# Lightning attention and a highway layer: weights loaded through an f32 staging tile late in the queue, five more idle products, and a re-written order

## The chip, the cores and the metric

The kernel runs on one core of one Trainium2 chip. The metric is the device time of one execution in microseconds (us), lower is better.

## What is computed

The reference is a block-wise decayed linear attention over `q`, `k`, `v` of shape (4 batches, 8 heads, 768 positions, 64) in f32, followed by a highway layer with two 512x512 weights. Cut to what matters:

```
for b in range(nb):                                  # blocks of 64 positions
    intra = (qb @ kb^T * Dmask) @ vb
    inter = (qb * lam_pow) @ kv_state
    out[block] = intra + inter
    kv_state = lam_block * kv_state + (kb * rev_pow)^T @ vb
x = out, heads side by side                          # 3072 x 512
H = relu(x @ w_h);  T = sigmoid(x @ w_t + b_t)
result = T * H + (1 - T) * x
```

## The kernel before

The work is cut into 12 steps (4 batches of 3 stretches of 256 positions; `n` is the step). The decay powers are folded into the operands: q is multiplied by `pow_q`, v by `pow_k`, both made once from `lam`. Each step has an attention part and a highway part.

Attention part of step n: q, k and v arrive as f32 by SyncE's queue (`load`, line 200; each DMA moves 256 KB, so a step has six). Three tasks bring them to bf16: `cast_k` (kinds `ck2`, `ck`), `scale` for q (`cq2`, `cq`) and for v (`cv2`, `cv`). TensorE turns k and q over (`trans`, `tr2`/`tr`, products with the identity, line 218), an engine copies the turned tile out of PSUM (`evac_h`, `et2`/`et`), TensorE makes scores (`scores`, `s`, line 234) in two halves u = 0, 1, VectorE masks them (`mask`, `m`, line 238), TensorE multiplies by v (`intra`, `a`, line 259), keeps the running state (`state`, `kv`, line 267; copied out by `ss`), and adds the state's share (`inter`, `i0`/`i`, line 247). `xT` copies the result out. Steps 0 and 1 are cut in two parts of four heads each (the kinds with a 2 at the end).

Highway part: `block` (kind `f`, line 288) multiplies by the weights `w_b` in bf16, eight products of 128x256 a task, four tasks a step; `hx`, `g` and `thD`/`thP` combine; `turn` (`x`, line 310) turns the result back by products with the identity, `eo` copies it out and `st` stores it.

Nothing is scheduled on the fly. The kernel makes a list of tasks in a fixed order, each of a kind with an engine (table `KINDS`, or for copies a letter of the strings in `EN`: A is ScalarE, V VectorE, G GpSimd), and the list `ORDER` says in which order they are issued. Every engine runs its tasks strictly in that order. Line 436 asserts that no task stands ahead of one that it depends on. PSUM is shared: the tag "w" has five buffers (`WB`) for turned tiles, scores, highway products and turned-back results; "o" and "kv" have one each. The f32 staging tiles of q, k and v have five buffers each from step 2 on (`LA`).

Two things around the change. First, the idle products: `fill` (line 191) issues two products of the identity with itself, 128x512 each, into the attention's PSUM tile; nothing reads them. There are `NF` = 12 such tasks; all stand at the head of TensorE's queue, before the first turn of step 0. Second, the weights: `load_w` (line 164) issues from GpSimd a DMA that reads f32 and writes bf16, half the columns of one weight each. There are four (kind `gw`); the kind `lw` is empty here. In `ORDER` three of them stand at the head of GpSimd's queue and the fourth behind step 0's `cv2` tasks. SyncE's queue begins: step 0 (six DMAs), q of step 1's first half, q of step 2, the rest of step 1, the rest of step 2, step 3, and so on, with no weight among them.

Of the kernel before, what the change touches and what calls it, by code (L numbers as in the profile page):

```python
# [8 lines left out]
F32 = mybir.dt.float32  # L9
# [11 lines left out]
class Task:  # L21
# [9 lines left out]


LETTER = dict(A="ACT", V="DVE", G="POOL")
KINDS = {"SP": "lw l l2 st st1 st3", "DVE": "m hx hx1 hx4 thD thD1 thD4 btc", "POOL": "gw thP thP1 thP4", "ACT": "g g1 g4 pow tab", "PE": "bt fill tr tr2 kv i i0 s a f f1 f4 x x1 x3"}
FIXED = {kind: eng for eng, kinds in KINDS.items() for kind in kinds.split()}
LA = 5
XB = 3
OB = 12
WB = 5
NF = 12  # L40
PARTS = 2
TH = ["DVE", "POOL"]
GROUPS = [[0], [1], [2], [3], [4], [5], [6], [7], [8], [9], [10]]
EN = dict(
    ck2="AVGV", cq2="GVGG", cv2="GGGG", et2="AVAAVAAA", ss="VAVVVAVAAVVAVVVAVAAA", xT="VAAAVAAVAAAAAAAAVVVAAAAV",
    eo="AVVAAAAVAAVVAVAVVAVVAV", ck="AAAGGAGAAA", cq="GGGGGGGGGG", cv="GGGGVGGGGG", et="AAAVAVAAAVAAAAAAAVAA", eo1="A", eo3="VA")
ORDER = [
    25, 26, 12, 36, 13, 24, 14, 0, 34, 15, 6, 8, 35, 16, 17, 18, 75, 2, 19, 9, 20, 125, 28, 21, 22, 74, 23, 29, 27, 32, 84, 33,
    39, 30, 31, 85, 37, 44, 38, 40, 41, 45, 4, 78, 42, 76, 43, 46, 82, 86, 47, 83, 128, 48, 124, 49, 126, 50, 77, 10, 1, 132, 56,
    51, 88, 133, 11, 80, 5, 52, 81, 55, 79, 92, 57, 99, 53, 93, 87, 3, 100, 89, 90, 54, 101, 91, 94, 127, 95, 7, 98, 102, 130,  # L50
    103, 163, 96, 129, 131, 104, 97, 105, 162, 58, 106, 107, 137, 59, 134, 164, 108, 135, 138, 63, 203, 139, 136, 64, 140, 110,
    109, 202, 141, 60, 111, 142, 65, 61, 166, 243, 143, 66, 62, 113, 112, 165, 67, 204, 115, 144, 114, 145, 168, 170, 116, 167,
    146, 242, 171, 169, 71, 68, 147, 206, 172, 244, 69, 72, 177, 153, 173, 178, 176, 179, 205, 117, 180, 280, 174, 210, 181, 154,
    151, 182, 246, 211, 183, 281, 208, 184, 175, 148, 209, 185, 207, 282, 250, 152, 149, 118, 186, 119, 251, 245, 320, 212, 150,
    121, 213, 187, 155, 217, 122, 214, 216, 218, 215, 321, 247, 220, 219, 188, 221, 248, 189, 222, 191, 361, 283, 249, 190, 156,
    223, 192, 157, 284, 255, 322, 252, 224, 286, 256, 225, 193, 253, 287, 257, 399, 233, 285, 194, 226, 234, 195, 254, 360, 227,
    323, 290, 258, 159, 291, 259, 196, 324, 160, 362, 288, 260, 197, 326, 289, 231, 327, 364, 439, 328, 232, 261, 329, 292, 295,
    199, 325, 293, 296, 398, 228, 262, 200, 263, 368, 297, 229, 271, 402, 400, 369, 230, 330, 294, 298, 331, 266, 272, 299, 363,
    440, 300, 264, 267, 235, 335, 265, 301, 438, 365, 332, 268, 269, 302, 336, 303, 366, 333, 479, 236, 442, 337, 367, 406, 270,
    334, 237, 370, 480, 338, 407, 239, 371, 273, 339, 304, 240, 340, 403, 309, 401, 478, 305, 274, 310, 404, 373, 275, 405, 73,  # L60
    341, 374, 311, 443, 342, 375, 446, 343, 276, 408, 312, 447, 372, 376, 277, 409, 441, 377, 482, 306, 238, 378, 344, 307, 278,
    351, 345, 201, 410, 308, 279, 352, 379, 411, 313, 241, 413, 444, 481, 380, 161, 346, 414, 483, 445, 198, 381, 349, 158, 415,
    347, 486, 70, 350, 382, 487, 123, 348, 412, 120, 448, 383, 353, 416, 484, 449, 417, 317, 485, 418, 314, 354, 315, 318, 419,
    450, 316, 453, 420, 355, 384, 319, 451, 454, 356, 421, 389, 455, 385, 488, 390, 452, 386, 456, 429, 489, 457, 458, 357, 430,
    491, 358, 459, 387, 492, 359, 460, 493, 461, 424, 388, 422, 425, 391, 490, 423, 494, 462, 426, 495, 392, 427, 496, 393, 497,
    428, 394, 467, 498, 463, 431, 501, 512, 395, 502, 468, 499, 464, 396, 500, 503, 397, 469, 465, 432, 470, 466, 506, 504, 433,
    507, 471, 435, 505, 434, 515, 436, 513, 508, 516, 472, 437, 514, 475, 517, 473, 520, 476, 518, 474, 521, 523, 477, 509, 519,
    524, 522, 510, 525, 526, 511, 527, 528]


@with_exitstack
def kernel(
# [11 lines left out]
    nc = tc.nc  # L84
# [4 lines left out]
    DM = H * D  # L89
    KC = DM // 128  # L90
# [4 lines left out]
    singles = ctx.enter_context(tc.tile_pool(name="singles", bufs=1))  # L95
# [32 lines left out]
    id_f = singles.tile([KC, KC], F32)  # L128
    nc.vector.tensor_copy(id_f, id128[0:KC, 0:KC])
    bt_col = singles.tile([128, KC], F32)  # L130
    w_b = [singles.tile([128, KC, DM], BF16, name=f"w_b{i}") for i in range(2)]
    wh, wt = w_b

# [5 lines left out]
    def buf(name, tag, shape, dtype=BF16, bufs=1, pool=None):  # L139
        made[name] = Tile(tag, bufs)  # L140
        made[name].make = lambda: (pool or sb).tile(shape, dtype, tag=tag, name=tag, bufs=bufs)
        return made[name]
# [7 lines left out]
    def task(kind, emit, reads=(), writes=(), after=(), only=()):  # L150
        eng = FIXED.get(kind)
        if eng is None:
            i = count.get(kind, 0)
            count[kind] = i + 1
            eng = LETTER[EN[kind][i]]
        t = Task(kind, eng, emit, [made[x] for x in reads], [made[x] for x in writes], after, only)
        tasks.append(t)
        return t

    V, A, P, T = nc.vector, nc.scalar, nc.gpsimd, nc.tensor  # L160
    ENG = {"DVE": V, "POOL": P}


    def load_w(w, y):
        nc.gpsimd.dma_start(out=w_b[w][:, :, y * 256:(y + 1) * 256],
                            in_=(moe_w_h, moe_w_t)[w].rearrange("(kc p) n -> p kc n", p=128)[:, :, y * 256:(y + 1) * 256])

    def copy(eng, dst, src):
        if eng == "ACT":
            A.activation(dst, src, AF.Copy)  # L170
        else:
            ENG[eng].tensor_copy(dst, src)  # L172

    w_done = {}
    for y, w in ((0, 0), (0, 1), (1, 0), (1, 1)):
        a = task("gw", lambda eng, w=w, y=y: load_w(w, y))
        w_done[w, y] = [task("lw", lambda eng: None, after=[a])]


    def powers(eng):  # L180
# [14 lines left out]
    buf(("fill",), "o", [128, 2, NP, C], F32, pool=ps)  # L195
    for i in range(NF):
        task("fill", fill, writes=[("fill",)])
# [81 lines left out]
    def group(n, b):  # L279
        for g in GROUPS:  # L280
            if n in g:
                return g[0], 2 * (n - g[0]) + b, 2 * len(g)
        return n + b, 0, 1
# [39 lines left out]
    for n in range(N):  # L323
        bt, c = divmod(n, NST)
        P2 = n < PARTS
        parts = [slice(0, 4), slice(4, 8)] if P2 else [slice(0, 8)]
        y = "2" if P2 else ""
# [58 lines left out]
        for b in range(2):  # L386
            g, r, z = group(n, b)
            y = {1: "1", 2: "", 4: "4"}[z]
# [9 lines left out]
            w = 1 if z == 4 else 2  # L398
# [24 lines left out]
            y = "3" if fin else "1"  # L423
# [45 lines left out]
```

## Time and profile before

| | |
|---|---|
| median of 3 runs | 119.93 us (119.2 to 120.29) |
| profiled execution, its own time | 120.29 us |
| its span, first to last instruction of the program | 118.2 us |
| TensorE busy (matmul) | 104.4 us, 88% of the span |
| VectorE / ScalarE / GpSimd busy | 79.8 / 71.0 / 65.0 us |
| moved by DMA | 26.52 MB, mean 224 GB/s |
| mean granted TensorE clock | 0.907 |

In profile lines PE is TensorE's matmul, PEld its weight load, DVE VectorE, ACT ScalarE, POOL GpSimd and SP SyncE; a q behind an engine's name is its instruction queue. A line number such as L234 is a line of the kernel above. In group lines the tile behind `<-` is what is read, `x16` is the number of instructions. PEclk is the share of TensorE's full clock that was granted.

### The profile page before, as it was taken

To read this page: it belongs to the slowest core of one execution; us is meant where nothing else is said; L and a number is where in the kernel's file an instruction comes from. 1 tells how busy PE (TensorE), PEld (TensorE's weight loads), DVE (VectorE), ACT (ScalarE), POOL (GpSimd) and SP (SyncE) were. 2 spreads that over 40 slices of the span, in tenths; PEclk is the share of its full clock that TensorE was granted. 3 is DMA by queue.
4 is the path that set the end of the run, shared out by engine and by line. 5 is a ranking of instruction groups with operands and counts; after the bars stand their busy time and mean duration, and the time that the engine had idled before them with its cause. 6 is when DMAs were issued, how large, how long until landed. Compare 5 with 4: busy or idle time off the path is not lost.

```text
span 118.2 us, 4773 instructions
## 1 busy us (share of the span) xinstructions
PE 104.4 (88%) x2073; PEld 87.0 (74%) x2073; DVE 79.8 (67%) x131; ACT 71.0 (60%) x128; POOL 65.0 (55%) x57
## 2 busy tenths in 40 slices
PE   5983226998999999999999999999999999999960
PEld 1432114776888988989989889889898888889950
DVE  0112324494396899898977779798899868795840
ACT  3564222363706975876978975968697866237650
POOL 7793034937400799998098999849463001230620
PEclk9998555555699999999999999999999999999997
DMA  0999999999999999999999999506494422022373
GB/s 19 272 214 216 242 260 298 284 279 296 286 295 290 290 291 287 288 286 294 284 271 293 303 295 288 178 24 243 168 371 179 175 105 89 6 89 89 119 284 134
DMA packets 43900, 26.52 MB, mean 224 GB/s; under 512 B 1764, under 2 KB 40936, under 8 KB 43880
## 3 DMA queue, kind: packets, MB, share of 16 engines
q1 hardware_dynamic: 41616, 25.17, 76.7%
q0 software_dynamic: 2112, 1.05, 6.6%
q8 instruction: 16, 0.26, 0.9%
q14 instruction: 4, 0.03, 0.1%
q10 hardware_dynamic: 152, 0.01, 0.1%
HBM read 20.98 MB, written 6.29 MB: 231 GB/s over the span
## 4 chain that ended last, share of the span: by engine, by line
PE 78%; DMA 9%; SPq 3%; POOL 2%; DVE 1%; ACT 1%; issue 1%; POOLq 1%
PE w L288 37%; PE w L218 11%; DMA qf<-in_q_dram 9%; PE w L310 9%; PE w L234 6%; PE o L259 5%; PE kv L267 5%; PE o L247 5%; SPq L203 3%; POOL qb L212 2%; POOLq L464 1%; DVE m L238 1%; ACT kT L170 1%; DVE hmx L292 0%; DVE ss L172 0%
## 5 line engine op out<-in xcount | busy, mean ns | idle before, releaser
L288 PE MATMUL w<-xT,w_b 128*128 128x256 bf16 (+1 forms) x416 | 47.6, 265 | 0.0
L288 PEld LDWEIGHTS <-w_b 128*128 128x128 bf16 x416 | 36.6, 98 | 4.7 <-issue 0.2
L238 DVE TENSOR_TENSOR m<-w,tri 128x512 bf16<-128x512 f32 x48 | 31.1, 684 | 6.2 <-PE w L234 6.0
L304 POOL TENSOR_TENSOR th<-t_sb,hmx 128x512 bf16<-128x512 bf16 (+1 forms) x13 | 14.0, 1079 | 33.2 <-DVE hmx L292 17.4
L212 POOL TENSOR_TENSOR qb<-qf,pow_q 128x1024 bf16<-128x1024 f32 (+1 forms) x13 | 22.1, 1702 | 9.7 <-DMA qf<-in_q_dram 6.5
L212 POOL TENSOR_TENSOR vs<-vf,pow_k 128x1024 bf16<-128x1024 f32 (+1 forms) x13 | 21.2, 1636 | 5.7 <-issue 3.2
L292 DVE SCALAR_TENSOR_TENSOR hmx<-w,xT 128x512 bf16<-128x512 f32 (+1 forms) x26 | 16.7, 647 | 5.8 <-PE w L288 4.3
L301 ACT ACTIVATE w<-w,bt_col 128x256 f32<-128x256 f32 (+1 forms) x26 | 11.2, 432 | 10.7 <-PE w L288 5.6
L170 ACT ACTIVATE kT<-w 128x1024 bf16<-128x1024 bf16 (+1 forms) x13 | 12.0, 925 | 6.6 <-PE w L218 6.6
L170 ACT ACTIVATE xT<-o 128x512 bf16<-128x512 f32 x17 | 9.5, 598 | 8.0 <-PE o L259 6.9
L310 PE MATMUL w<-id,th 128*128 128x128 bf16 x96 | 12.8, 219 | 0.6 <-POOL th L304 0.6
L234 PE MATMUL w<-qT,kT 64*64 64x128 bf16 x384 | 12.6, 234 | 0.7 <-ACT kT L170 0.7
L170 ACT ACTIVATE qT<-w 128x1024 bf16<-128x1024 bf16 (+1 forms) x9 | 7.9, 881 | 8.6 <-PE w L218 8.6
L310 PE MATMUL w<-id,xT 128*128 128x128 bf16 x96 | 12.8, 220 | 0.0
L218 PE MATMUL w<-id,qb 128*128 128x128 bf16 x96 | 8.7, 238 | 4.4 <-DVE qb L212 2.2
L301 ACT ACTIVATE t_sb<-w,bt_col 128x256 bf16<-128x256 f32 (+1 forms) x26 | 10.5, 457 | 2.1 <-PE w L288 2.0
L304 DVE TENSOR_TENSOR th<-w,hmx 128x512 bf16<-128x512 f32 (+1 forms) x13 | 8.3, 647 | 4.0 <-ACT w L301 3.6
L218 PEld LDWEIGHTS <-qb 128*128 128x128 bf16 x96 | 6.7, 106 | 5.6 <-POOL qb L212 2.6
L218 PE MATMUL w<-id,kb 128*128 128x128 bf16 x96 | 8.8, 238 | 1.7 <-ACT kb L170 1.5
L259 PE MATMUL o<-m,vs 64*64 64x128 bf16 x384 | 9.1, 233 | 1.1 <-DVE m L238 1.1
L310 PEld LDWEIGHTS <-th 128*128 128x128 bf16 x96 | 9.4, 98 | 0.8 <-POOL th L304 0.8
L234 PEld LDWEIGHTS <-kT 64*64 64x64 bf16 x384 | 8.5, 113 | 2.0 <-ACT kT L170 0.9
(45 smaller groups left out, 124.8 us busy)
## 6 DMA issues: line engine op xcount, KB each, us to landing
qf<-in_q_dram SPq DMA_DIRECT2D x24, 256.0 KB, 5.5
vf<-in_v_dram SPq DMA_DIRECT2D x24, 256.0 KB, 5.4
kf<-in_k_dram SPq DMA_DIRECT2D x24, 256.0 KB, 5.3
out_dram<-o_sb SPq DMA_DIRECT2D x23, 256.0 KB, 2.4
w_b<-in_moe_w_h_dram POOLq DMA_DIRECT2D x2, 256.0 KB, 8.3
w_b<-in_moe_w_t_dram POOLq DMA_DIRECT2D x2, 256.0 KB, 10.3
out_dram<-o_sb SPq DMA_DIRECT2D x2, 128.0 KB, 1.7
lam_bc<-in_lam_dram ACTq DMA_DIRECT2D x1, 4.0 KB, 3.5
```

Of the source, the lines that this page charges most:

```text
L170: A.activation(dst, src, AF.Copy)
L212: ENG[eng].tensor_tensor(dst[:, hs], in0=get(x, n, p).rearrange("p h (j d) -> p h j d", j=J), in1=pw[:, :, :, None].to_broadcast([128, hs. ...
L218: T.transpose(get(x + "tr", n, p)[:, i, j, :], get(x + "b", n)[:, j, h:h + 2, :], id128)
L234: T.matmul(get("s", n, u, e)[half(b), i, j, :], lhsT=turned("k", n)[half(e), hp, b * C + j:(b + 1) * C:J], rhs=turned("q", n)[half(e), hp, ...
L238: V.tensor_tensor(get("m", n, u)[:, e], in0=get("s", n, u, e), in1=tri[:, None].to_broadcast([128, 2, J, C]), op=ALU.mult)
L247: T.matmul(get("o", n)[half(e), b, hp, :], lhsT=get("ss", n, b)[half(e), hp, :], rhs=turned("q", n)[half(e), hp, b * C:(b + 1) * C], start ...
L259: T.matmul(get("o", n)[half(e), b, 2 * u + i, :], lhsT=get("vs", n)[half(b), 4 * u + 2 * i + e, j, :], rhs=get("m", n, u)[half(b), e, i, j ...
L288: T.matmul(get(x, g, js[0])[:, i, :], lhsT=w[:, kc, j * 128:(j + 1) * 128], rhs=get("xT", g)[:, kc, :], start=(kc == 0), stop=(kc == KC - 1))
L292: V.scalar_tensor_tensor(get("hmx", g, js[0]), in0=get("h", g, js[0]), scalar=0.0, in1=get("xT", g)[:, js[0]:js[-1] + 1, :], op0=ALU.max, ...
L301: A.activation(get(*gate(g, js))[:, i, :], get("t", g, js[0])[:, i, :], AF.Sigmoid, bias=bt_col[:, j:j + 1])
L304: ENG[TH[js[0] // len(js) % 2]].tensor_tensor(get("th", g)[:, js[0]:js[-1] + 1, :], in0=get(*gate(g, js)), in1=get("hmx", g, js[0]), op=AL ...
L310: T.matmul(get("x", n, b, p)[:, (j - js[0]) * 128:(j - js[0] + 1) * 128], lhsT=get(x, g)[:, j, r * C:(r + 1) * C], rhs=id128, start=(j == ...
```

## The change

The GpSimd DMAs go. Each weight is loaded as f32 into a staging tile `w_f` by four SyncE DMAs of 256 KB (128 partitions, two of four row blocks, half the columns), and eight tasks of kind `cw` copy the pieces to `w_b`: four on GpSimd, three on ScalarE, one on VectorE. In the new `ORDER` the eight loads stand on SyncE's queue behind all of steps 0, 1 and 2 and ahead of step 3.

`NF` is 17. Twelve idle products stand ahead of the first turn as before; the five others stand on TensorE's queue behind each of the four turns of step 0 and behind the first scores of step 0.

`ORDER` and the strings of `EN` are written anew throughout. For steps 0 and 1 the loads of SyncE are in the order v, k, q, q, k, v (step 0), q, k, k, q, v, v (step 1), then step 2. On GpSimd the first tasks are now step 0's second `cv2` and step 1's `cq2`, `ck2`, `cq2`; VectorE has `ck2`, `cv2`, `cq2`, `cq2` of step 0 at its head, and the `cv2` tasks of step 1 between the masks of step 0 and those of step 1.

The diff, the numbers of `ORDER` left out:

```
-KINDS = {... "SP": "lw l l2 st st1 st3", ... "POOL": "gw thP thP1 thP4", ...}
+KINDS = {... "SP": "lw l l2 st st1 st3", ... "POOL": "thP thP1 thP4", ...}
-NF = 12
+NF = 17
 EN = dict(
-    ck2="AVGV", cq2="GVGG", cv2="GGGG", et2="AVAAVAAA", ss="VAVVVAVAAVVAVVVAVAAA", xT="VAAAVAAVAAAAAAAAVVVAAAAV",
-    eo="AVVAAAAVAAVVAVAVVAVVAV", ck="AAAGGAGAAA", cq="GGGGGGGGGG", cv="GGGGVGGGGG", et="AAAVAVAAAVAAAAAAAVAA", eo1="A", eo3="VA")
+    cw="GVGGGAAA", ck2="VVGA", cq2="VVGG", cv2="VGVV", et2="VAAVAVAV", ss="AAVAAAAVAVAAAAVVAVAV", xT="VAVAAAAAAAAAAAAAAAAAAAAA",
+    eo="AVVAAAVAAVAVAVAAAAVAVA", ck="VAAGGAGVGG", cq="GVGGGGGGGG", cv="GGGGGGGGGG", et="AVAVAVVAVAAAAAAAAAAA", eo1="A", eo3="AA")
...
+    w_f = [singles.tile([128, KC, DM], F32, name=f"w_f{i}") for i in range(2)]
     w_b = [singles.tile([128, KC, DM], BF16, name=f"w_b{i}") for i in range(2)]
...
-    def load_w(w, y):
-        nc.gpsimd.dma_start(out=w_b[w][:, :, y * 256:(y + 1) * 256],
-                            in_=(moe_w_h, moe_w_t)[w].rearrange("(kc p) n -> p kc n", p=128)[:, :, y * 256:(y + 1) * 256])
+    def piece(x, y, i):
+        return x[:, 2 * i:2 * i + 2, y * 256:(y + 1) * 256]
+
+    def load_w(w, y, i):
+        nc.sync.dma_start(out=piece(w_f[w], y, i), in_=piece((moe_w_h, moe_w_t)[w].rearrange("(kc p) n -> p kc n", p=128), y, i))
...
     for y, w in ((0, 0), (0, 1), (1, 0), (1, 1)):
-        a = task("gw", lambda eng, w=w, y=y: load_w(w, y))
-        w_done[w, y] = [task("lw", lambda eng: None, after=[a])]
+        w_done[w, y] = []
+        for i in range(2):
+            a = task("lw", lambda eng, w=w, y=y, i=i: load_w(w, y, i))
+            w_done[w, y].append(task("cw", lambda eng, w=w, y=y, i=i: copy(eng, piece(w_b[w], y, i), piece(w_f[w], y, i)), after=[a]))
```

## The prediction

> **What bounds the kernel now.** I read the page first (busy shares, the 40 slices), then the windows, the chain of waits over the first 33 us, and the timeline there.
>
> ```profile
> PE   5983226998999999999999999999999999999960
> PEclk9998555555699999999999999999999999999997
> DMA  0999999999999999999999999506494422022373
> ```
>
> A slice is 2.96 us. From the eleventh slice to the last but two TensorE has no gap; before that it is mostly empty and at half clock, while the DMA engines are full from 3 us to 77 us. The windows, cut where the clock changed (columns: window, length, busy time and instructions of PE, PEld, DVE, ACT, POOL, clock, DMA share, GB/s):
>
> ```profile
> 7.59:11.01 3.42, 1.28 (x19) 0.70 (x21) 0.69 (x1) 1.40 (x3) 2.41 (x3) 1.00 1.28 214
> 11.01:14.42 3.41, 1.05 (x20) 0.54 (x16) 1.08 (x3) 0.60 (x1) 0.00 (x0) 0.50 1.27 238
> 14.42:17.83 3.41, 1.19 (x12) 0.73 (x15) 1.24 (x3) 0.60 (x1) 1.03 (x1) 0.50 1.23 256
> ...
> 21.25:24.66 3.41, 3.41 (x52) 2.53 (x56) 2.15 (x5) 1.70 (x3) 3.36 (x4) 0.50 1.08 284
> 24.66:28.07 3.41, 2.92 (x80) 2.47 (x74) 2.11 (x4) 2.38 (x4) 0.91 (x2) 0.50 1.04 280
> 28.07:31.49 3.42, 3.42 (x73) 2.76 (x66) 1.71 (x3) 1.46 (x2) 2.96 (x2) 0.50 1.13 295
> ```
>
> The clock was full until 11.0, half until 31.5, then full to the end. A window with PE busy 1.28 of 3.42 cost it; 3.41 of 3.41 in 21.25 to 24.66 did not yet bring it back. The chain names what the start waits for:
>
> ```profile
> 5.13 10.95 DMA qf<-in_q_dram
> 16.17 1.04 POOL qb L212
> ...
> 21.18 1.03 PE w L218 x8
> ...
> 32.24 0.35 PE w L234 x16
> ```
>
> A load of q for step 1, issued at 5.13, lands at 16.09. Between 5 and 18 us the four weight DMAs land too (10.59, 13.08, 15.47, 17.98 in the trace); they read 2 MB f32 in all. So steps 0 and 1 are starved by weights that no product reads before 30.9 us. Step 1's last load lands at 23.39, step 2's at 27.14, step 3's at 32.35.
>
> So the end is fixed by when TensorE becomes dense at full clock. From step 2's first scores (32.17) to the end of the span (118.24) it is 86.1 us, with one block of L288 (eight products, 0.87 in the chain) already done. The new order does that block later, so its span is the time of step 2's first scores plus 86.1 + 0.9 = 87.0, plus whatever is run at half clock behind them. The products are otherwise the same.
>
> **The change, part by part.** The sum is made against the profiled execution: span 118.24 and 2.05 around it, 120.29. The median 119.93 is 0.36 below that; I subtract 0.36 at the end.
>
> *Loads moved.* Without weights in front, loads land at the spacing that the trace has when loads are alone: 21.66, 22.53, 23.39, 24.23, so 0.87 us for 256 KB. The first lands at 5.16 as before. Then step 0 is complete at 9.5 (was 13.67), step 1 at 14.7 (was 23.39), step 2 at 19.9 (was 27.14), the eight weight pieces at 20.8 to 26.9, step 3 at 32.1 (was 32.35). From step 3 on the bytes ahead are equal, so nothing is lost there: SyncE has eight issues more, which cost 0.4 to 0.8 each and run while its queue waits for the full DMA engines. GpSimd loses four issues, 0.94 + 0.75 + 0.75 + 0.80 = 3.2 us, which stood ahead of its first casts.
>
> *Casts added.* Eight of 128x512 f32 to bf16. The rows for that shape (kb): GpSimd 0.61, ScalarE 0.63, VectorE 0.43, and 1.09 where GpSimd worked beside it. So GpSimd 2.4, ScalarE 1.9, VectorE 0.4 to 1.1. They stand between 21 and 28 us. The first highway block needs ScalarE's two (pieces landed at 20.8 and 21.7, done by about 25), and I have TensorE there at 25 to 27; the others are done at 23 to 28 and asked for at 28 or later. On the path: 0 (covered by the attention of step 2), up to 1 if that cover is gone. Behind the waiting ScalarE casts stand `xT` of step 1 and `ss` of step 2, 0.6 and 0.4; both have the same cover.
>
> *Idle products.* 24 of them took 6.7 us before; at full clock the later ones run at 0.21, so a `fill` of two is 0.43 and five are 2.15. They go into gaps that TensorE has anyway while ScalarE and VectorE copy (0.6 to 0.69 a copy). Walking the four turns: turns and fills alternate from 8.1 (end of the twelve) to 11.1, where the first scores start; without them about 10.2. Then the masks of step 0 and landings of step 1 (11.2 to 14.7) take over. Price on the path: 0 to 1, taken in the walk below.
>
> *The walk to step 2's first scores*, in row durations (VectorE: mask 0.64, turned tile 0.69 or 1.22, scale 0.69, copy of xT 0.69, ss 0.42; ScalarE 0.60, 1.02 and 0.38). At full clock: scores u=0 at 11.1, u=1 at 12; four masks on VectorE 11.75 to 14.35; `a` of step 0 at 14.6; one `et2` and two `cv2` that VectorE now does, and xT, to 17.2; `kv`, `ss`, `i0`, `kv` to 17.1; scores of step 1 at 17.2; its two `kv`, each waiting for an `ss`, to 19.7; `i` at 20.6; second scores 21.1; VectorE's cast of k for step 2, 20.4 to 21.5; turns 21.8 to 22.8; the turned tiles 23.0 to 24.2; scores of step 2 at 24.4. At half clock from 14.4 on, L218 x4 is 0.61 instead of 0.28, L234 0.64 instead of 0.35, L259 1.07 instead of 0.57, and the same walk ends at 26.5. The cast of k (128x1024 on VectorE) has no row: twice the 128x512 rows is 0.86 to 2.17; I took 1.1, since GpSimd is busy beside it for only a part; so -0.2 to +1.1.
>
> *The clock.* This is the unknown. Bounds: full throughout, 24.4 + 87.0 = 111.4 span; or half from 14.4 until TensorE has been dense for a while. From 26.5 on it is dense, and half clock does about 0.54 of full (0.61 / 0.28, 1.07 / 0.57, 0.64 / 0.35), so each microsecond behind 26.5 costs 0.46. Back at 28.1 (one dense window) costs 0.7, at 31.5 (as before) 2.3: span 114.2 to 115.8. By my walk PE is busy 1.9 of 3.4 us in 11.0 to 14.4 and about 2 in the next two windows. That is nearer to the 1.28 that lost the clock than to the 3.4 that has always held or won it, so I take the loss, and a return at about 30, cost 1.6: 26.5 + 87.0 + 1.6 = 115.1, with 0.4 for VectorE's cast 115.5. Plus 2.05 is 117.6, less 0.36 is 117.2; I take 117.0, as the fall may also come one window later.
>
> The page "TensorE: Matmul & The Clock Gate" of the Trainium skill says in "Why this matters for your kernels" that the clock falls after idle gaps over about 3 us. The row here disagrees: before 11.0 the longest gap of PE was 1.45 us, and it fell. By the page's rule the new order (no gap over 2 us) would keep the clock and end at 113.1; but its "Part 4: PE-mode transpose" adds that turns do not count as busy, which speaks against these fillers being enough.
>
> *The rest of the run.* GpSimd, with step 3's v landing at 32.1 and its 1.90 a scale, has step 4's v ready at 39 (asked for at 42) and step 6's at 50 (asked for at 55). Engine loads over the remaining 85 us are as before: VectorE gives up 5 copies of xT and 3 of o and takes turned tiles; nothing there is over 10 in 10.
>
> **The rivals.** *A, forecast:* clock lost, regained around 28 to 31.5: 115.5 to 118.5. *B: the idle products hold the clock.* For it: PE's share in the two windows behind them rises from 1.28 and 1.05 to about 3.0 and 1.9. Against: the windows from 14.4 to 21 have no idle product. 111.4 + 0.8 (cast beside GpSimd) + 2.05 - 0.36 gives 113.9, 113.1 without. *C: the early gain is given back by a less dense run.* Before, PE is busy for 78.51 of 78.51 us from 34.9 on, in another order; the new one has VectorE fuller in its early part (my count: 12 us of VectorE work beside 10 of PE between step 0's masks and the first highway blocks). If 3 us of gaps stand there or later, about 120: no change. *D, slower:* the clock does not come back until far later, because the highway blocks wait for weights that now arrive last, and TensorE never fills a window. The price is 0.46 per us beyond 31.5; 117.6 + 0.46 x 7.9 = 121.2, so it decides from a return at about 39.4 on, 8 us after the last weight piece and cast. Against it: at 28 all weights are there, and step 0 to 2's twelve blocks (10 us) wait for nothing. *E: nothing changes*, since the end follows the DMA engines: against it, the last loads land at 76 and the end is 42 us behind.
>
> **How the numbers follow.** A 0.48, B 0.25, C 0.14 (118.7 to 121.1), D 0.11 (over 121.1), E 0.02. A measurement of this kernel tells about 1% from no change: faster is below 118.7, slower above 121.1. Faster 0.48 + 0.25 = 0.73, same 0.16, slower 0.11. The likeliest, A, is 117.0, its own range 115.5 to 118.5. The 8 in 10 range takes A, nearly all of B and half of C: 112.8 to 120.2.
>
> **What would show it.** Right: step 1's last load lands by 15.5 and its first scores start by 19; step 2's first scores at 24 to 27; the weights land last; PE without gaps from 28 on. The clock row tells A from B: half in 14 to 31, or 1.00 throughout. Wrong: PE idle beside `cw`, scores of step 2 after 29, a half clock past 35, or gaps of PE behind 35 us.

## The result, and the profile after

The changed kernel takes 111.84 us (median of 4, 111.7 to 112.25), the kernel before 120.11 beside it. The ratio is 0.9327, interval 0.9266 to 0.9388: faster by 6.7%. Times here and below are medians of all executions, while ratios and their intervals go by the fast executions of both kernels. The forecast was 117.0 with a range of 112.8 to 120.2. Direction and cause of most of it were right; the time lies 1.0 us below the range.

The page of the changed kernel, the lines that answer to the three shown of before:

```profile
PE   4999877579999999999999999999999999999960
PEclk9999999999999999999999999999999999999999
DMA  0999999999999999999999999999997340024264
```

A slice is now 2.76 us. The empty part of TensorE's line is gone but for five slices between 11 and 25 us that are five to eight tenths busy, and no slice is at half clock. The DMA engines are full until about 83 us (74 before). The windows, cut at the boundaries of this execution's clock (columns as before: length, PE, PEld, DVE, ACT, POOL, clock, DMA share, GB/s):

```profile
8.28:11.69 3.41, 3.41 (x43) 1.95 (x41) 2.28 (x5) 1.20 (x2) 1.86 (x2) 1.00 1.21 291
11.69:15.10 3.41, 2.46 (x75) 1.79 (x73) 3.41 (x6) 1.32 (x3) 1.78 (x3) 1.00 1.22 291
15.10:18.52 3.42, 2.58 (x88) 2.12 (x90) 3.42 (x8) 2.14 (x5) 1.49 (x1) 1.00 1.20 292
18.52:21.93 3.41, 1.94 (x54) 1.58 (x56) 2.21 (x5) 0.59 (x1) 0.76 (x2) 1.00 1.02 278
21.93:25.34 3.41, 2.74 (x76) 2.35 (x72) 3.21 (x5) 2.79 (x6) 2.38 (x3) 1.00 1.06 353
...
34.90:105.00 70.10, 69.86 (x1573) 62.40 (x1571) 53.39 (x86) 51.93 (x99) 47.83 (x33) 1.00 0.82 243
```

The first row is the one with four of the five idle products: PE is busy for all of it, where the kernel before had 1.28 of 3.42. The clock stays full through four windows in which TensorE is busy for 1.94 to 2.74 us only. The last row: behind 35 us TensorE is idle for 0.24 us only (for none before).

What the start waits for now, from the timeline (start, length, engine, line, instruction, and in brackets the idle time before it and who ended it):

```profile
18.74 0.41 PE L239 MATMUL w<-qT,kT 64*64 64x128 bf16 x12
19.87 0.69 DVE L175 CAST kb<-kf 128x1024 bf16<-128x1024 f32 x1 [1.20 <-DMA kf<-in_k_dram]
20.62 0.62 PE L223 MATMUL w<-id,kb 128*128 128x128 bf16 x8 [1.48 <-DVE kb L175]
21.59 1.91 POOL L217 TENSOR_TENSOR vs<-vf,pow_k 128x1024 bf16<-128x1024 f32 x1 [2.65 <-DMA vf<-in_v_dram]
22.26 1.24 ACT L173 ACTIVATE w_b<-w_f 128x512 bf16<-128x512 f32 x2
23.00 0.42 PE L239 MATMUL w<-qT,kT 64*64 64x128 bf16 x16 [0.55 <-DVE qT L175]
```

Step 1's second scores end at 19.15; then TensorE waits for k of step 2. Step 2's scores start at 23.00, and the span ends at 110.2: 87.2 us later, where the prediction had 87.0. The chain of waits names the last of step 2's loads on SyncE's queue, v:

```profile
14.91 6.54 DMA vf<-in_v_dram
21.45 0.02 issue
...
21.59 1.92 POOL vs L217
...
23.54 0.44 PE kv L272 x16
```

GpSimd scales v for 1.92 us, and step 2's first state products start at 23.54, just behind the scores. So k (by way of the scores) and v (by way of these products) are nearly tied: in this order an earlier k alone would gain little.

### The profile page after: what moved, and what is told of

It reads as the page before. It is cut to its first block, busy times and chain, and to the rows that moved or that the text cites. A ratio compares the mean times of both kernels' runs of the same rounds, so it can differ in the third digit from the quotient of the medians.

```text
span 110.2 us, 4797 instructions
## 1 busy us (share of the span) xinstructions
PE 100.9 (91%) x2083; PEld 84.4 (77%) x2083; DVE 78.5 (71%) x128; ACT 73.2 (66%) x137; POOL 63.9 (58%) x55
## 4 chain that ended last, share of the span: by engine, by line
PE 71%; SPq 12%; DMA 6%; POOL 5%; issue 1%; DVE 1%; POOLq 1%; ACT 0%
PE w L293 37%; SPq L208 12%; PE w L315 9%; PE w L223 8%; DMA vf<-in_v_dram 6%; PE o L264 5%; PE w L239 4%; PE kv L272 4%; PE o L252 3%; POOL vs L217 2%; POOL qb L217 2%; POOL kb L175 1%; DVE hmx L297 1%; POOLq L469 1%; ACT o_sb L173 0%
## 5 line engine op out<-in xcount | busy, mean ns | idle before, releaser
L217 POOL TENSOR_TENSOR vs<-vf,pow_k 128x1024 bf16<-128x1024 f32 (+1 forms) x11 | 20.0, 1824 | 12.5 <-DMA vf<-in_v_dram 12.4
L309 POOL TENSOR_TENSOR th<-t_sb,hmx 128x512 bf16<-128x512 bf16 (+1 forms) x13 | 15.0, 1155 | 20.3 <-DVE hmx L297 13.3
L217 POOL TENSOR_TENSOR qb<-qf,pow_q 128x1024 bf16<-128x1024 f32 (+1 forms) x11 | 19.2, 1746 | 6.5 <-PE kv L272 2.6
L173 ACT ACTIVATE xT<-o 128x512 bf16<-128x512 f32 x22 | 12.2, 597 | 2.4 <-PE o L264 2.2
L173 ACT ACTIVATE kT<-w 128x1024 bf16<-128x1024 bf16 (+1 forms) x11 | 10.0, 908 | 5.7 <-PE w L223 5.7
L173 ACT ACTIVATE o_sb<-w 128x512 f32<-128x512 f32 (+1 forms) x17 | 9.7, 576 | 4.8 <-PE w L315 4.6
L198 PE MATMUL o<-id 128*128 128x512 bf16 x34 | 10.0, 439 | 1.4 <-POOL id masks.py:199 1.4
L272 PE MATMUL kv<-vs,kb 64*64 64x64 bf16 x320 | 9.4, 194 | 0.4 <-DVE ss L175 0.3
L315 PEld LDWEIGHTS <-xT 128*128 128x128 bf16 x96 | 9.3, 98 | 0.5
L223 PE MATMUL w<-id,kb 128*128 128x128 bf16 x96 | 7.7, 220 | 1.9 <-DVE kb L175 1.5
```

The costliest lines, as they stand in the source:

```text
L217: ENG[eng].tensor_tensor(dst[:, hs], in0=get(x, n, p).rearrange("p h (j d) -> p h j d", j=J), in1=pw[:, :, :, None].to_broadcast([128, hs. ...
L223: T.transpose(get(x + "tr", n, p)[:, i, j, :], get(x + "b", n)[:, j, h:h + 2, :], id128)
L272: T.matmul(get("kv", n // NST)[half(e), hp, :], lhsT=get("kb", n)[half(b), j, 2 * hp + e, :], rhs=get("vs", n)[half(b), 2 * hp + e, j, :], ...
L309: ENG[TH[js[0] // len(js) % 2]].tensor_tensor(get("th", g)[:, js[0]:js[-1] + 1, :], in0=get(*gate(g, js)), in1=get("hmx", g, js[0]), op=AL ...
L315: T.matmul(get("x", n, b, p)[:, (j - js[0]) * 128:(j - js[0] + 1) * 128], lhsT=get(x, g)[:, j, r * C:(r + 1) * C], rhs=id128, start=(j == ...
```

## The experiments

Two theories at first. Theory 1: the five idle products hold the clock, and that is most of the gain. Theory 2: the loads are, since steps 0 to 2 no longer share the DMA engines with the weights. Kernels were run in three groups, each on a chip of its own with the kernel before beside it (119.88, 119.90 and 119.88 us).

### The changed kernel without the five idle products

```
-NF = 17
+NF = 12
```

and the five left out of `ORDER`.

> The changed kernel without its five extra idle products; every other task keeps its place. Theory 1 (the idle products hold the clock): TensorE's clock falls to half at 11 to 15 us and returns at 28 to 32; the scores of step 2 come at 25 to 26.5 instead of 23.0 and some 0.7 to 2.3 us are lost behind them, so 115 to 117 us. Theory 2 (the loads are what counts; the denser start holds the clock by itself): the clock stays full and the time is 111 to 112 us, up to 0.9 below the changed kernel, because the first scores start up to 0.9 us earlier.

Measured: 113.24 us (112.38 to 114.45), ratio 0.9405 (0.9319 to 0.9491). Clock lost, as theory 1 had it; time lost, 0.8 to 1.4 us by the medians against the two groups in which the changed kernel ran (the intervals overlap), nearer to theory 2. The windows of this kernel:

```profile
9.21:12.62 3.41, 1.54 (x43) 0.94 (x40) 3.17 (x6) 1.26 (x3) 2.65 (x3) 1.00 1.22 290
12.62:16.03 3.41, 2.83 (x63) 2.49 (x65) 2.91 (x5) 1.55 (x3) 1.08 (x2) 0.50 1.22 290
16.03:19.45 3.42, 3.37 (x82) 2.79 (x79) 2.35 (x5) 1.34 (x3) 1.90 (x1) 0.50 1.20 297
19.45:22.86 3.41, 3.41 (x63) 3.04 (x61) 2.71 (x6) 1.40 (x3) 0.90 (x1) 0.50 1.06 328
22.86:26.27 3.41, 2.72 (x79) 2.41 (x76) 3.30 (x5) 2.59 (x7) 2.11 (x3) 1.00 1.09 343
```

Half clock for 10.24 us, and the slower products mostly fill what would be gaps: 2.83, 3.37 and 3.41 busy, where the changed kernel has 2.46, 2.58 and 1.94 in about the same places. Step 2's scores come at 24.08 instead of 23.00. Three executions with the same mean clock (0.953 to 0.954) took 112.38, 112.73 and 113.76, so the share of half clock alone does not set the price.

### The changed kernel with its weights loaded early

The eight tasks `lw` stand in `ORDER` behind the first four loads of step 0.

> The changed kernel with its eight f32 weight loads put behind the first four loads of step 0 on SyncE's queue instead of behind step 2; idle products and casts keep their places. Theory 1 (the idle products alone hold the clock): full clock through the start; step 2's last load lands at about 28 instead of 21.5, the scores of step 2 come at about 29 to 30, and with 87 us behind them the time is 118 to 119. Theory 2 (the loads decide both): the gap in which TensorE waits for step 1 also costs the clock in spite of the idle products; scores of step 2 at 29 to 31 and 1.5 to 4 us more at half clock, 119.5 to 123.

Measured: 117.78 us, ratio 0.9813 (0.9749 to 0.9877), 5.3 to 5.9 above the changed kernel (112.46 and 111.84 in its two groups). The place of 2 MB in the queue alone is worth that much in this order. In the chain two loads stand for the start, the first of them a weight's:

```profile
4.91 5.23 DMA w_f<-in_moe_w_h_dram
20.97 6.46 DMA vf<-in_v_dram
...
27.57 1.92 POOL vs L217
```

Step 2's scores came at 29.02, and 86.9 us later the span ended (115.9). TensorE had nothing at all from 11 to 14 us and lost the clock for 6.8 us, idle products or not; that was over at 21.2, before it could cost much. That is close to theory 1's number (118 to 119), but the gap did cost the clock, as theory 2 had it.

### The kernel before with five more idle products

```
-NF = 12
+NF = 17
```

and the five in `ORDER` behind the four turns of step 0 and its first scores.

> The kernel before with five more idle products, behind each turn of step 0 and behind its first scores, nothing else changed. Theory 1: if idle products alone hold the clock, it stays full and the 20.5 us at half clock go: TensorE waits for loads until 21 us either way, and the work between 21 and 31.5 shrinks by about half of its 10 us, so 114 to 116. Theory 2: the waits of 1.5 to 2.5 us between 12 and 18 us are too long for five products, the clock falls one or two windows later and is back at 28 to 32, 119 to 121, no change.

Measured: 120.67 us, ratio 1.0056 (1.0023 to 1.0089). No gain; a loss of half a per cent. The clock fell at 15.5 instead of 11.0 and was back at 32.5. Idle products alone did nothing for this start, which waits for loads.

### The kernel before with late weights

The four tasks `gw` stand in `ORDER` behind GpSimd's `cq2` of step 1, second half.

> The kernel before with its four weight DMAs moved on GpSimd's queue behind the cast of q for step 1 (second half), so that they are issued at about 14 to 18 us; 12 idle products as before. Steps 0 and 1 then land without weights among them. Theory 1: the clock still falls at 11 to 15 for want of idle products; step 1 starts 6 to 8 us earlier but runs at half clock, 115 to 118. Theory 2: the earlier loads keep TensorE busy enough, full clock, 111 to 114.

Measured: 115.71 us (114.93 to 116.59), ratio 0.9636 (0.9546 to 0.9726). One moved group of DMAs gives 4.2 of the 8.1 us, with the clock at half from 12.0 to 29.0.

### Both in the order of before

> The kernel before with both: weight DMAs behind the cast of q for step 1 and five more idle products at the places where the changed kernel has them; the rest of the order as before. It had 115.7 with the late weights alone. Theory 1 (idle products and load order make up the whole gain, the rest of the order does not matter): 111.5 to 113. Theory 2 (the rest of the order is worth 2 to 3 us): the idle products give the 1 to 1.5 us that they give in the changed kernel, 114 to 115.5.

Measured: 115.48 us (115.07 to 115.76), ratio 0.9609 (0.9541 to 0.9677), against 115.71 without the idle products: no difference that can be told, though the clock now falls for 3.4 us only in the profiled execution. So 3.0 to 3.6 us lie in what is left of the change: the rest of the order and the queue of the weights. The timeline on GpSimd shows a part of it:

```profile
15.23 1.04 POOL L212 TENSOR_TENSOR qb<-qf,pow_q 128x512 bf16<-128x512 f32 x1 [0.16 <-DMA qf<-in_q_dram]
16.22 1.68 POOL L165 DMA_DIRECT2D w_b<-in_moe_w_h_dram  x2
17.89 1.50 POOL L165 DMA_DIRECT2D w_b<-in_moe_w_t_dram  x2
19.37 3.93 POOL L212 TENSOR_TENSOR vs<-vf,pow_k 128x512 bf16<-128x512 f32 x3
```

GpSimd issues four DMAs for 3.2 us and only then scales v of step 1, for which step 1's state update waits (L267 at 20.51, 1.90 idle before it). In the changed order VectorE scales it, at 14.46. The kernel before has its issues at the head of GpSimd's queue and at 9.19, so this wait comes with the place that the experiment gave them; with another place the late weights might give more than 4.2.

### The order of the change, weights by GpSimd DMAs

The changed kernel with `load_w` and `w_done` of before, no `w_f`, no `cw`; the four DMAs behind the cast of q for step 1.

> The changed kernel with its order and its 17 idle products, but with the weights as before the change: four GpSimd DMAs that write bf16, no f32 tile, no casts. They are issued behind the cast of q for step 1, at about 14 to 18 us, so still behind the loads of steps 0 and 1. Theory 1 (how the weights are converted does not matter, only when they are loaded): 111.5 to 112.5, as the changed kernel. Theory 2 (the GpSimd DMAs themselves cost): four issues of 0.75 to 0.94 stand ahead of q and v of step 2 on GpSimd, and the weights share the DMA engines with step 2's loads, so step 2's scores come 1.5 to 3 us later, 113.5 to 115.

Measured: 113.94 us (113.78 to 115.39), ratio 0.951 (0.9425 to 0.9595); 1.5 to 2.1 above the changed kernel (112.46 and 111.84 in its two groups), as theory 2 had it. Its chain at the start:

```profile
14.96 8.57 DMA vf<-in_v_dram
...
23.67 1.91 POOL vs L212
```

The same load took 6.54 in the changed kernel, and step 2's scores came at 24.52 instead of 23.00. The weight DMAs run on a queue of their own beside SyncE's, and v of step 2 shares the DMA engines with them; on SyncE's queue it stands ahead of them. Whether the conversion on the way costs anything by itself was not separated.

### Two of the five idle products

Kept: those behind the fourth turn and the first scores.

> The changed kernel with two of the five idle products kept, behind the fourth turn of step 0 and behind its first scores. In the runs so far every window of 3.41 us with TensorE busy for 1.83 us or less was followed by half clock, and every one with 1.94 or more at full clock by full clock. Theory 1 (the busy share of such a window decides): the two add 0.9 to the 1.54 us of the run without them, the clock holds, 111.6 to 112.2. Theory 2 (the longest gap or the number of products decides): the clock falls as without them, 112.4 to 114.5.

Measured: 114.83 us (113.01 to 115.83), ratio 0.9586 (0.9498 to 0.9673). Theory 1 of that run falls: the rule by TensorE's busy share was wrong. The time is above theory 2's range too (112.4 to 114.5), and 1.6 above the kernel with none of the five, which ran in another group. Why is not known; in the two profiles the half clock lies later here, from 14.70 to 24.95 against 12.62 to 22.86. The window that lost the clock:

```profile
11.29:14.70 3.41, 2.13 (x74) 1.69 (x73) 3.10 (x6) 1.50 (x3) 2.24 (x3) 1.00 1.20 290
```

2.13 of 3.41 lost it here; 1.94 kept it in the changed kernel.

### The five idle products on a quarter of the array

```
+    def fill_q(eng):
+        for i in range(2):
+            T.matmul(get("fill")[0:64, i], lhsT=id128[0:64, 0:64], rhs=id128[0:64, None, :].to_broadcast([64, NP, 128]), start=True, stop=True)
...
-        task("fill", fill, writes=[("fill",)])
+        task("fill", fill if i < 12 else fill_q, writes=[("fill",)])
```

Since busy time did not tell the windows apart, I counted array work from the records of products: columns streamed times the share of the 128x128 array in use, each product in the window in which it ends. A 128x512 product takes 0.21 us at full clock, so a window of 3.41 us holds 16 of them, 8,192 columns at most.

> The changed kernel, but its five extra idle products use 64 of 128 rows and 64 of 128 columns of the array: as many instructions, as many columns streamed, a quarter of the array. Theory 1 (the clock goes by array work: columns streamed times the share of the array in use; in all ten profiles a half-clock window with 2,560 such columns or less stayed at half, one with 3,008 or more of the 8,192 possible ended it): the five give 1,280 instead of 5,120, the window behind the first 12 is at about 2,400 + 600 to 1,000 and falls in most executions, 112.5 to 115. Theory 2 (busy time decides): as the changed kernel, full clock, 111.6 to 112.3.

Measured: 112.3 us (111.73 to 113.91), ratio 0.9362 (0.9298 to 0.9426); the changed kernel itself had 112.46 (112.29 to 114.07), ratio 0.9385 (0.9333 to 0.9437), in this group. A miss for theory 1: the clock held in most executions. The two windows:

```profile
9.09:12.51 3.42, 3.42 (x43) 1.68 (x44) 1.72 (x3) 1.23 (x3) 2.62 (x3) 1.00 1.22 290
12.51:15.92 3.41, 2.47 (x75) 1.89 (x72) 3.39 (x6) 1.19 (x2) 1.14 (x2) 1.00 1.22 290
```

By my count they hold 3,072 and 3,056 columns. The first is about what I had expected (2,400 + 600 to 1,000), but I had expected a fall there. Windows of 2,688 to 3,328 columns have gone both ways, so this run does not tell the two measures apart. Open.

### The changed kernel once more

> The changed kernel once more, so that the others of this call stand beside it on the same chip. Expected by all theories: 111.5 to 112.3, clock full in most executions.

Measured as just given: 112.46, and a miss on the clock. All six executions had 4 to 7 us at half clock (mean clock 0.969 to 0.98); four took 112.29 to 112.55, the other two 113.97 and 114.07. In the first group three had none and took 111.70, 111.71 and 111.97. So the clock is at the edge, and in most executions a fall costs about half a microsecond, as far as two chips can be compared.

The one with a profile is that of 113.97, and it shows a dear fall: half clock from 21.49 to 28.31, where TensorE has become dense. The first sixteen highway products, here and in the chain of the changed kernel at full clock:

```profile
24.46 3.60 PE L293 MATMUL w<-xT,w_b 128*128 128x256 bf16 x16
```

```profile
23.98 1.85 PE w L293 x16
```

The span is 112.2 instead of 110.2. So these 6.8 us at half clock cost 2.0 us, while the 10.24 us from 12.62 on in the kernel without the five idle products cost 0.4 (spans 110.6 and 110.2, what the missing products save included). Where the half clock lies counts more than how long it is.

### Each cast twice

`copy(...)` of `cw` done twice.

> The changed kernel with each of its eight casts of a weight piece done twice: 2.4 us more on GpSimd, 1.9 on ScalarE, 0.4 on VectorE, all between 22 and 30 us. Theory 1 (the casts are hidden beside the attention of step 2, as the prediction had them): 111.8 to 112.5. Theory 2 (ScalarE's two casts release the first highway block at 23.5 and are on the path): at least 1.24 us more on ScalarE ahead of that block, 112.8 to 114.

Measured: 113.26 us (113.18 to 113.81), ratio 0.9468 (0.9414 to 0.9523), 0.8 above the changed kernel beside it; the intervals overlap, but its four executions lie above the four of 112.29 to 112.55. ScalarE:

```profile
22.90 2.47 ACT L173 ACTIVATE w_b<-w_f 128x512 bf16<-128x512 f32 x4
...
25.42 0.83 PE L293 MATMUL w<-xT,w_b 128*128 128x256 bf16 x6 [0.39 <-ACT w_b L173]
```

1.24 us more on ScalarE make the first highway block wait for 0.39 us in this profile, and 0.8 reach the end by the medians; GpSimd's and VectorE's doubled casts may have a part in that. Single, ScalarE's two end at 23.50, and TensorE has the scores and state products of step 2 until 23.98, so there they cost nothing.

### Two versions meant to be faster

Weights ahead of step 2's loads, and the highway blocks of steps 0 and 1 ahead of step 2's turns:

> A version meant to be faster than both: the changed kernel with the eight weight loads ahead of step 2's loads on SyncE's queue, and the highway blocks of steps 0 and 1 with their casts ahead of step 2's turns on all engines; the turned-back results of step 0 stand between step 2's turns and scores. Theory 1 (what bounds the start is the bytes that must land before TensorE has enough to do: 12 loads, then a weight quarter at a time): the blocks start at about 19 us instead of 24, and 1.5 to 2.5 us of the 4 us that TensorE now idles between 11 and 24 go, 109.5 to 110.5. Theory 2 (copies on ScalarE and VectorE bound the start, or step 2 now lands too late): 111.5 to 113.5.

Measured: 120.37 us (118.64 to 120.93), ratio 0.9966 (0.9911 to 1.0022). The idea was not tried fairly: in the order that I wrote by hand ScalarE's cast for the next block stood behind a `g` that waited for an earlier block, and between 23 and 40 us TensorE was busy for only 2.49, 1.83 and 2.49 of 3 us, then 2.65 and 1.65 of 4. This order is worth nothing; whether the loads' order would be worth something with all engines ordered for it stays open.

Three more idle products in gaps (behind the first `kv` of step 0, the second scores and `a` of step 1), into buffers of the tag "w":

> A version meant to be faster than both: the changed kernel with three more idle products, in gaps of TensorE: behind the first state update of step 0, behind the second scores of step 1 (where TensorE waits 1.5 us for k of step 2) and behind step 1's product with v. Theory 1 (the windows at 15 to 22 us, with 2,688 and 2,976 columns of array work, are near the edge and fall in some executions; 1,024 more each holds them): full clock in all, 111.4 to 111.9, and less spread. Theory 2 (the gaps are not free: products delay turns and scores, and PSUM buffers come free later): 112 to 113.

Measured: 112.03 us (111.84 to 113.64), ratio 0.9355 (0.931 to 0.94), against 112.46 (ratio 0.9385, 0.9333 to 0.9437) beside it. All but one of its seven executions lie between 111.84 and 112.09 at a mean clock of 0.993 to 1; the other, at half clock from 19.89 to 23.31, took 113.64. The intervals overlap, so a gain is not shown; a loss is not either.

## Why the prediction was wrong

**The bound: right.** The end is step 2's first scores plus 87 us. In the profiles of the changed order with full clock behind these scores it is 86.5 to 87.7 (23.00 and 110.2; 29.02 and 115.9; 24.05 and 111.2 with doubled casts); with half clock behind them it was 88.8 (23.46 and 112.2).

**Loads moved: right in kind, and the largest term.** Step 1 was complete at 15.12 (14.7 forecast), step 2 at 21.45 (19.9), the last weight at 27.36 (26.9). Step 2 is 1.6 late mainly because 2.05 us instead of 0.87 pass between its second q (16.87) and its first k (18.92); why is not known. The early place of the loads is worth 4.2 us in the old order and 5.3 to 5.9 in the new one.

**Casts: right.** 0 on the path was forecast, up to 1 if the cover is gone. Single they cost nothing on ScalarE; doubled they cost 0.8, so the cover named (the attention of step 2) is just long enough.

**Idle products: right in their price** (first scores at 11.01 with them, 10.59 without; up to 1 was forecast, and other profiles with all five have 10.79 to 12.03).

**The clock: the step that failed.** "I take the loss, and a return at about 30, cost 1.6" stood on top of a walk that lost 2.1 by half clock. That is 3.7 us, 3.5 of the 5.2 by which the forecast missed, since 0.2 was taken off at its end. The clock was not lost in the profiled execution, nor in two of the other three. And where it was lost, both prices were too high: without the five products step 2's scores came at 24.08, not 26.5, and the clock was back at 22.9, not 30. The walk added the longer products to the path; the windows show that they ran mostly in time in which TensorE would have waited for loads or for VectorE. The measured price is 0.5 to 1.4 us by the medians in place of 3.7, and 2.0 in the one profile in which the fall came as late as 21.49. There 4.85 us at half clock behind step 2's scores cost 1.5, or 0.32 a microsecond; 0.46 was forecast, for a stretch of that kind. Even with the clock lost the kernel without the five products took 112.4 to 114.5, below rival A's 115.5.

**The walk at full clock: 1.4 us too late**, which put rival B at 113.1 to 113.9 and the low end of the range at 112.8. So B, which had the clock right, would have missed too. The first sign is on VectorE:

```profile
11.46 2.48 DVE L243 TENSOR_TENSOR m<-w,tri 128x512 bf16<-128x512 f32 x4 [0.74 <-PE w L239]
...
14.46 1.38 DVE L217 TENSOR_TENSOR vs<-vf,pow_k 128x512 bf16<-128x512 f32 x2
...
15.71 0.25 PE L239 MATMUL w<-qT,kT 64*64 64x128 bf16 x3
```

The four masks end at 13.94 (14.35 forecast), most of `a` of step 0 starts at 14.00 (14.6), and step 1's scores start at 15.71 (17.2). The walk had them behind VectorE's copy of xT and behind both state products of step 0; they started before that copy (15.78) and among those products. VectorE's cast of k took 0.69, below both ends that I had scaled from the 128x512 rows (0.86 to 2.17), so the 0.4 added for it was not needed. From there on TensorE waited mainly for loads: 1.48 us for the cast of step 2's k, which had itself waited 1.20 for its load.

**What was not priced by itself: the rest of the order.** The walk was made in the new order, so its worth is in the 24.4, but the prediction gives no share to it. Going from before to after, by medians against the same kernel before: late weights 119.9 to 115.7; idle products to 115.5; the other order to 113.9; weights on SyncE's queue behind step 2's loads to 111.8 (112.5 in the other group). The last two, 3.0 to 3.6 us together, are 40 to 45% of the gain. That the other order gains by taking GpSimd's issues from ahead of v of step 1 is what the chain of that kernel suggests; it was not run alone, and the experiment itself had put the issues there. The prediction counted GpSimd's 3.2 us of issues as a relief, but the first cast behind them (6.20 before) waited for `pow_q`, not for them.

**Two small readings** cost nothing: the nines of the DMA row before end at 74 us, not 77, and by the three pairs named half clock does 0.46 to 0.55 of full, not about 0.54.

**The clock's rule.** The Trainium skill ("TensorE: Matmul & The Clock Gate", "Part 1: The HAM clock gate") says that the clock is judged in free-running windows of 3,413 ns. The runs agree: falls and returns lie whole multiples of 3.41 us apart (11.0 and 31.5 before; 12.62 and 22.86 without the idle products), and the first boundary differs from run to run. Its advice in "Why this matters for your kernels", no idle gaps above about 3 us, does not suffice here. The longest gap ahead of the fall at 11.0 was 1.45 us:

```profile
9.80 0.40 PE L218 MATMUL w<-id,kb 128*128 128x128 bf16 x4 [1.45 <-ACT kb L170]
```

The changed kernel kept the clock with a gap of 1.48 (the line at 20.62 above).

## What to carry to other kernels

While the start waits for loads, count bytes: whatever no product needs yet goes behind what the next product needs, on the same queue, since a second queue takes its share of the DMA engines at once (v of step 2 took 8.57 us beside one, 6.54 without). A half TensorE clock eats idle time first, and only what is left over reaches the end: 10.24 us of it cost 0.4 in the thin start, 6.8 us cost 2.0 where TensorE was dense. When an issue or a copy leaves an engine, ask what stood behind it.

## What the runs showed of the hardware

Which window loses the clock is not settled by TensorE's busy time: 1.94 of 3.41 us kept it, 2.13 lost it. By array work, as counted above, 34 of the 35 half-clock windows ahead of 45 us in fourteen profiles fall on two sides: at 2,656 of 8,192 columns or fewer half clock went on (21 windows), from 3,008 on it ended (13); one with 3,072 went on. This depends on the count: with each product in the window in which it starts, the sides overlap (one window of 2,640 ended it, one of 2,816 and two of 3,072 did not). For the loss the two outcomes overlap either way: by the count above the lowest window that kept the clock had 2,688, the highest that lost it 3,328. I take array work for the better guess, which is not shown; the run made to separate it from busy time did not.
